# An attention and token-MLP kernel: the opening in pieces of 128 tokens, with two of its eight tiles transposed by DMA

## The chip, the cores and the metric

The kernel runs on one core of one Trainium2 chip. The metric is the device time of one execution in microseconds (us); lower is better. TensorE (PE) multiplies matrices, VectorE (DVE) and ScalarE (ACT) do element-wise work and reductions, GpSimd (POOL) clears buffers and issues transfers, SyncE (SP) issues transfers only. SP, ACT and POOL each have a queue of transfers; all queues are served by the same 16 DMA engines of the core.

## What is computed

Four layers in a row: twice an attention block and a token-mixing MLP, each with a layer norm in front and a residual sum behind.

```python
x = A_x                                              # (1, 2048, 1024) bf16
x = x + _A_ref(_layernorm(x), A_wqkv, A_wo)          # attention
x = x + _B_ref(_layernorm(x), B_w1, B_b1, B_w2, B_b2)  # token MLP
x = x + _A_ref(_layernorm(x), A_wqkv, A_wo)
x = x + _B_ref(_layernorm(x), B_w1, B_b1, B_w2, B_b2)

# _A_ref: H = 32 heads of 32, W = 8 keys a query, dilation 2
idx = pos[:, None] - (jnp.arange(W) * 2)[None, :]    # keys at s, s-2, ..., s-14
logits = einsum("bhsd,bhswd->bhsw", q, k[..., idx, :]) * Dh ** -0.5
attn = softmax(where(idx >= 0, logits, -1e9))
o = einsum("bhsw,bhswd->bhsd", attn, v[..., idx, :]) @ wo

# _B_ref: mixes along the 2048 tokens
u = gelu(einsum("bsd,sf->bdf", h, w1) + b1);  y = einsum("bdf,fs->bds", u, w2) + b2
```

## The kernel before

The dilation of 2 splits the 2048 tokens into two classes, even and odd tokens, which never meet in the attention. Each class has 1024 tokens: eight tiles of 128 tokens (NT = 8), or two halves of 512 (HT). The attention of a class needs the normalized input transposed, with features on the partitions: `hT[c][hf]` holds class c, token half hf, so tiles 0 to 3 of class 0 are in `hT00` and tiles 4 to 7 in `hT01`.

The change touches the opening of the first attention layer. There the eight class-0 tiles of x are loaded (`x_stage`, L247: even tiles on SP's queue, odd tiles on ACT's) into buffers called gg. For each tile, DVE computes mean and variance (`moments`, L264), ACT the reciprocal root (`rsqrt`, L197), DVE normalizes in place (`norm`, L273); for tile 4, called `own`, ACT does all of it (`own_sum`, `own_square`, `norm_act`). TensorE then turns the tile in eight transpositions of 128x128 into a PSUM bank (`turn`, L287) and DVE or ACT copies it into hT (`place`, L292). Matmuls on the identity (`idle`, L258) fill TensorE's time before there is work. The program order of TensorE, DVE, ACT and POOL in this opening is written out by hand in `first_tiles` (L251); SP's order follows from when each transfer is asked for.

A projection is one unit of `project(c, part, dt, hf)` (L407): part 0, 1 or 2 for q, k or v, dt one of eight groups of 128 features, hf the token half. It is eight matmuls of 128x512 over the features (or over fewer columns, `lo` to `hi`, when called in pieces), and then an ACT copy into q, k or v. Its weights are loaded on SP's queue when the first unit asks (`weights`, L378). In the hand-written part, half 0 of k 0, k 1, q 0, q 1, k 2 and k 3 is projected, then half 1 of k 0, k 1, q 0 and q 1. Half 1 is the first reader of hT01.

After the opening, `qk` (L440) multiplies q by the shifted k on DVE, 4096 elements per partition at a time, into a tile T, and TensorE sums each head with a selection matrix (`qk_sum`, L475) into the bank sc. For the first head group (n = 0) the four T's of a pair are each followed by their own sums. When all sums of a group are there, `softmax_front` (L485) and `softmax_back` (L495) run on ACT and DVE; the probabilities go through DRAM to be spread over partitions (`spread`), and `pv` multiplies them with v.

The eight class-1 tiles are loaded by POOL into the same gg buffers, each into one that held a class-0 tile: tile i of class 1 takes the place of tile (i + 7) mod 8 of class 0 (`staged`, L243). So the first of them waits for TensorE's transposition of tile 7. They are normalized by DVE (even) and ACT (odd) and transposed by DMA on SP's queue (`to_hT`, L240). The biases b1 and b2 of the MLP are loaded by POOL (`load_biases`, L156), two bytes at a time, ahead of these tiles; they are used only in the MLP.

The rest is laid out by a planner, `weave` (L792): it walks through the attention's units in order, keeps an estimate of the time on TensorE and on DVE, and pulls units from fill streams ("second" for class 1's tiles, "v_ahead", "out0" and others) when TensorE would wait. A unit `("at", pe, dve)` sets the planner's two clocks, `("drain", name)` takes all that is left of a stream. These numbers only decide order.

Of the kernel before, what the change touches and what calls it, by code (L numbers as in the profile page):

```python
# [11 lines left out]
ALU = mybir.AluOpType  # L12
# [14 lines left out]
def kernel(  # L27
# [42 lines left out]
    AHEAD = 5.0  # L70
    assert D == H * DH and W == 8 and SC == 1024 and HD * KD == H and SB * CH == 32
# [67 lines left out]
    sel = const.tile([P, SB * DQ, 32], BF16, name="sel")  # L139
    nc.gpsimd.memset(sel[:], 0.0)  # L140
# [5 lines left out]
    maskc = const.tile([P, W, W], FP32, name="maskc")  # L146
# [4 lines left out]
    b1_bf = const.tile([P, FT], BF16, name="b1_bf")  # L151
    b2_bf = const.tile([P, NT, DIL], BF16, name="b2_bf")
    b1_sb = const.tile([P, FT], FP32, name="b1_sb")
    b2_sb = const.tile([P, NT, DIL], FP32, name="b2_sb")
# [92 lines left out]
    def x_stage(c, i):  # L247
        eng = nc.gpsimd if c else (nc.scalar if i % 2 else nc.sync)
        eng.dma_start(out=staged(c, i), in_=xin_v[c, i])

    def first_tiles(hT, project):  # L251
        tiles = [staged(0, i) for i in range(NT)]
        mv, rs, tps = {}, {}, {}
        s1, t1, nm, ss = (st(n, [P, w]) for n, w in (("s1", NDC), ("t1", 1), ("nm", 1), ("ss", 1)))
        junk = x2("junk")
        own = NT // 2

        def idle(n):  # L258
            ps = bank()
            for _ in range(n):  # L260
                nc.tensor.matmul(ps[:].rearrange("p (b t) -> p b t", t=P), lhsT=ident[:],
                                 rhs=ident[:].unsqueeze(1).to_broadcast([P, 4, P]), start=True, stop=True)

        def moments(i):  # L264
            s = st("bn", [P, NDC, 6])
            for n in range(NDC):
                nc.vector.bn_stats(out=s[:, n, :], in_=tiles[i][:, n * 512:(n + 1) * 512])
            mv[i] = st("mv", [P, 2])
            nc.vector.bn_aggr(out=mv[i][:], in_=s[:])
            rs[i] = st("rs", [P, 1])  # L270
            rsqrt(rs[i][:], mv[i][:, 1:2], 1.0, eps1)

        def norm(i):  # L273
            norm_dve(tiles[i], tiles[i], mv[i][:, 0:1], rs[i])

        def own_sum(n):
            nc.scalar.activation(out=junk[:, n * 512:(n + 1) * 512], in_=tiles[own][:, n * 512:(n + 1) * 512],
                                 func=ACT.Identity, accum_out=s1[:, n:n + 1])

        def own_square():  # L280
            nc.scalar.activation(out=t1[:], in_=s1[:, 1:2], func=ACT.Copy, scale=-1.0 / D)  # L281
            nc.scalar.activation(out=nm[:], in_=s1[:, 0:1], func=ACT.Identity, bias=t1[:], scale=-1.0 / D)
            nc.scalar.activation(out=junk[:], in_=tiles[own], func=ACT.Square, bias=nm[:], accum_out=ss[:])
            rs[own] = st("rs", [P, 1])
            rsqrt(rs[own][:], ss[:], 1.0 / D, eps1)

        def turn(i):  # L287
            tps[i] = psp.tile([P, KD, P], BF16, name="tp", tag="ps")
            for kt in range(KD):
                nc.tensor.transpose(tps[i][:, kt, :], tiles[i][:, kt * P:(kt + 1) * P], ident[:])  # L290

        def place(i, copy):  # L292
            copy(out=hT[0][i // 4][:, :, (i % 4) * P:(i % 4 + 1) * P], in_=tps.pop(i)[:])

        dve, act = nc.vector.tensor_copy, nc.scalar.copy
        idle(16)
        moments(0)
        own_sum(0)
        moments(1)
        norm(0)  # L300
        turn(0)
        idle(3)
        own_sum(1)
        moments(2)
        norm(1)
        turn(1)
        idle(5)
        place(0, act)
        moments(3)
        place(1, dve)  # L310
        norm(2)
        norm(3)
        banks = {}
        for u, i in (((1, 0), 2), ((1, 1), 3), ((0, 0), None)):
            banks[u] = bank()
            project(*u, 0, banks[u], 0, 2 * P)
            if i:
                turn(i)
        own_square()
        place(2, act)  # L320
        place(3, dve)
        norm_act(tiles[own], tiles[own], nm, rs[own])
        moments(own + 1)
        moments(own + 2)
        for n, u in enumerate(banks):
            project(*u, 0, banks[u], 2 * P, HT)
            if n == 0:
                turn(own)
                norm(own + 1)
                place(own, dve)  # L330
                moments(own + 3)
                norm(own + 2)
        for n, u in enumerate(((0, 1), (1, 2), (1, 3))):
            if n == 2:
                norm(own + 3)
            turn(own + 1 + n)
            place(own + 1 + n, dve)
            project(*u, 0, bank(), 0, HT)
        for u in ((1, 0), (1, 1), (0, 0), (0, 1)):
            project(*u, 1, bank(), 0, HT)  # L340

# [15 lines left out]
    class Attn:  # L357

        def __init__(self, li, hT, early):
            self.li, self.hT, self.early = li, hT, early  # L360
            self.oT = [[None] * KD for _ in range(DIL)]
            self.wts = {}
            self.pbs = {}
            self.prior = None

# [41 lines left out]
        def project(self, c, part, dt, hf, ps=None, lo=0, hi=HT):  # L407
# [5 lines left out]
            for kt in range(KD):  # L413
# [4 lines left out]
                nc.tensor.matmul(ps[:, lo:hi], lhsT=cols, rhs=self.hT[c][hf][:, kt, lo:hi], start=(kt == 0), stop=(kt == KD - 1))  # L418
# [21 lines left out]
        def qk(self, n, dq):  # L440
# [10 lines left out]
            for par in range(2):  # L451
                if not joined:
                    yield "dve", 2.2, ready, free if par else [], 0.0, 0.0
                    yield "pe", 0.6, [], [], 0.0
                T = self.t_buf(n, dq, par)
                mult = nc.vector.tensor_tensor(out=T, in0=q.unsqueeze(1).to_broadcast([P, 4, SC]),  # L456
                                               in1=window(k, par, 2, [(2, 4), (1, SC)]), op=ALU.mult)
# [4 lines left out]
                if not joined:  # L462
                    self.qk_sum(dq, par, T)
# [5 lines left out]

        def t_buf(self, n, dq, par):  # L470
            if self.li == 0 and 0 < n < 3:
# [76 lines left out]
        def stream(self, lead):  # L548
# [39 lines left out]
            if lead is not None:  # L588
                yield "drain", "second"
            yield "open", "v_ahead"  # L590
            for n in range(last + 1):
                done = self.early if n == NCQ else 0
                for half in range(2):
                    nx = (n + half, 1 - half)
                    turn = nx == (NCQ, 0) and self.li > 0
                    yield from self.qk(n, 2 * half)
                    yield from self.qk(n, 2 * half + 1)
                    if half:
                        yield from self.softmax_front()
                    if lead is not None and nx == (0, 1):  # L600
                        for u in ((0, 2, 1), (0, 3, 0), (0, 3, 1),):
                            yield from self.proj(0, *u)
                    elif nx[0] <= last and not turn:
# [188 lines left out]
    def weave(lead, fills, lags):  # L792
# [35 lines left out]
        for kind, *unit in lead:  # L828
# [3 lines left out]
            elif kind == "drain":  # L832
                while unit[0] in opened:
# [27 lines left out]
    for li in range(2):  # L861
# [9 lines left out]
        def opening():  # L871
            for i in range(NT):
                x_stage(0, i)
            load_biases()
            clear_pads()
            with tc.manual_schedule(engines={getattr(mybir.EngineType, e) for e in ("PE", "DVE", "Activation", "Pool")}):
                first_tiles(hT, partial(at_.project, 0))
                for i in range(NT):
                    x_stage(1, i)
            yield "at", 27.0, 29.0  # L880
            for u in ((1, 2, 1), (1, 3, 1), (0, 2, 0),):
                yield from at_.proj(0, *u)
# [75 lines left out]
```

## Time and profile before

| | |
|---|---|
| runs, us | 1280.4, 1280.18, 1280.54, 1280.45; median 1280.43 |
| the profiled execution | 1280.4 us, span 1278.6 us from first to last instruction |
| granted TensorE clock | 1.000 |
| DMA moved | 173.00 MB in 217,816 packets |

TensorE's operations in the opening, by line, with the mean time of one (starts lie closer than that, since matmuls are pipelined):

| line | what | count up to 40 us | mean ns |
|---|---|---|---|
| L261 | warm-up on the identity, 512 columns | 24 | 472 |
| L290 | transposition, 128 columns | 64 | 220 |
| L418 | projection, 256 columns | 48 | 273 |
| L418 | projection, 512 columns | 81 (7 to 40 us) | 379 |

Other operations of the first 60 us:

| what | where | us |
|---|---|---|
| half statistics of a tile, two of them | DVE L267 | 1.29 |
| aggregate | DVE L269 | 0.21 |
| normalize a tile | DVE L233 | 0.50 |
| copy a turned tile into hT | DVE L293 / ACT L293 | 0.69 / 0.99 |
| one multiply of q and k, 4096 elements | DVE L456 | 2.28 |
| copy of k or v, 1024 elements; of q, 512 | ACT L425; L422 | 1.00; 0.57 |
| issue of an x tile by POOL | POOL L249 | 0.54 |
| DMA transpose of a tile, issue to landing | SP L241 | 3.1 to 5.9, median 4.6 |

The profile's timeline lists, per engine, the start of a group of equal instructions, its length, engine, line, operation, tiles and count; in brackets the idle time before it and what ended that. L numbers are lines of the kernel. "PEld" is TensorE loading weights, "SPq" the issuing of transfers by SP. Busy TensorE is not TensorE at its peak.

### The profile page before, as it was taken

How to read it: one execution, taken by the hardware profiler on the slowest of the kernel's cores; microseconds unless marked ns; L12 is line 12 of the kernel's file. 1: busy time of each engine (PE TensorE's matmuls, PEld its weight loads, DVE VectorE, ACT ScalarE, POOL GpSimd, SP SyncE). 2: the span in 40 equal slices, each digit the busy share in tenths (PEclk: the TensorE clock that was granted, in tenths of full speed). 3: DMA queues.
4: the chain of work that ended last, by engine and by line, in shares of the span. 5: the costliest groups of instructions: out<-in, count | busy, mean ns of one | idle time of the engine just before them, and what ended most of it. 6: DMA issues, size and time to landing. Idle time of an engine off the chain costs nothing.

```text
span 1278.6 us, 15576 instructions
## 1 busy us (share of the span) xinstructions
PE 1265.0 (99%) x6284; PEld 577.5 (45%) x6284; DVE 689.9 (54%) x869; ACT 489.1 (38%) x812; POOL 61.0 (5%) x166
## 2 busy tenths in 40 slices
PE   8999999999999999999999999999999999999999
PEld 4344444444444444444444444444444444444444
DVE  6789999999114322334798834899930233111011
ACT  6845446634424533324533445453352343000000
POOL 3000001001000000000000000010010000000000
PEclk9999999999999999999999999999999999999999
DMA  9843454553422289953737642358262223344331
GB/s 256 189 124 102 103 139 143 169 144 115 132 83 83 62 233 294 294 159 87 185 105 200 153 124 81 82 156 208 66 181 83 81 67 93 103 129 134 99 115 52
DMA packets 217816, 173.00 MB, mean 135 GB/s; under 512 B 32080, under 2 KB 198352, under 8 KB 215696
## 3 DMA queue, kind: packets, MB, share of 16 engines
q1 hardware_dynamic: 206768, 126.11, 36.6%
q0 software_dynamic: 9248, 37.51, 10.4%
q10 hardware_dynamic: 1728, 8.39, 1.8%
q8 instruction: 49, 0.80, 0.3%
q14 instruction: 23, 0.19, 0.1%
HBM read 139.47 MB, written 26.21 MB: 130 GB/s over the span
## 4 chain that ended last, share of the span: by engine, by line
PE 76%; DVE 5%; issue 2%; ACT 1%; DVEq 0%
PE ps L719 30%; PE ps L743 29%; PE ps L418 11%; PE ps L664 4%; DVE T L456 2%; PE sc L480 1%; DVE pr L538 1%; DVE pr L543 1%; DVE xr L689 0%; ACT h L227 0%; ACT h L238 0%; DVE v L545 0%; DVE xr L692 0%; ACT ln L200 0%; DVE bn L207 0%
## 5 line engine op out<-in xcount | busy, mean ns | idle before, releaser
L719 PE MATMUL ps<-h,w 128*128 128x512 bf16 x1792 | 388.1, 379 | 2.0 <-ACT h L238 2.0
L743 PEld LDWEIGHTS <-w 128*128 128x128 bf16 x1820 | 177.8, 98 | 209.8 <-issue 2.1
L719 PEld LDWEIGHTS <-w 128*128 128x128 bf16 x1792 | 175.1, 98 | 214.2 <-issue 3.4
L418 PE MATMUL ps<-hT,wq 128*128 128x512 bf16 (+1 forms) x1112 | 241.7, 375 | 0.6 <-ACT t L281 0.4
L743 PE MATMUL ps<-g,w 128*128 128x512 bf16 (+1 forms) x1040 | 227.6, 376 | 0.0
L743 PE MATMUL ps<-gg,w 128*128 128x512 bf16 (+1 forms) x780 | 171.8, 376 | 0.0
L748 DVE SCALAR_TENSOR_TENSOR xr<-ps,b_sb,xr 128x512 bf16<-128x512 f32 (+1 forms) x65 | 45.5, 738 | 225.7 <-PE ps L743 193.7
L418 PEld LDWEIGHTS <-wq 128*128 128x128 bf16 x1112 | 109.0, 100 | 128.6 <-issue 8.8
L456 DVE TENSOR_TENSOR T<-q,k 128x4096 bf16<-128x4096 bf16 x44 | 99.0, 2285 | 70.2 <-ACT q L422 52.1
L543 DVE TENSOR_TENSOR pr<-pr 128x2048 bf16<-128x2048 bf16 (+1 forms) x128 | 119.4, 950 | 0.3
L730 DVE TENSOR_TENSOR tmp<-ps,gg 128x512 f32<-128x512 f32 x48 | 33.2, 692 | 150.2 <-PE ps L719 150.2
L418 PE MATMUL ps<-hT,wv 128*128 128x512 bf16 x448 | 100.3, 379 | 0.0
L664 PE MATMUL ps<-wo,oT 128*128 128x512 bf16 x384 | 89.1, 379 | 0.7 <-DVE oT L545 0.7
L425 ACT CAST k<-ps 128x1024 bf16<-128x1024 f32 x60 | 60.7, 1014 | 60.2 <-PE ps L418 58.8
L538 DVE TENSOR_TENSOR pr<-pb,v 128x2048 bf16<-128x2048 bf16 x64 | 75.9, 1218 | 10.8 <-ACT v L425 6.7
L538 DVE TENSOR_TENSOR pr<-pb,g 128x2048 bf16<-128x2048 bf16 x64 | 76.7, 1217 | 7.2 <-DMA pb<-pd 4.6
L418 PEld LDWEIGHTS <-wv 128*128 128x128 bf16 x448 | 48.8, 111 | 48.7 <-issue 4.2
L730 DVE TENSOR_TENSOR tmp<-ps,g 128x512 f32<-128x512 f32 x48 | 33.2, 692 | 49.7 <-PE ps L719 48.7
L664 PEld LDWEIGHTS <-oT 128*128 128x128 bf16 x384 | 37.4, 98 | 46.7 <-DVE oT L545 1.2
L422 ACT CAST q<-ps 128x512 bf16<-128x512 f32 x60 | 34.9, 584 | 49.5 <-PE ps L418 49.5
L731 ACT ACTIVATE gg<-tmp,b_sb 128x512 bf16<-128x512 f32 x48 | 34.6, 722 | 49.9 <-DVE tmp L730 49.9
L774 ACT COPY odd<-w 128x896 bf16<-128x896 bf16 x32 | 30.0, 937 | 55.9 <-DMA w<-in_B_w_dram 55.9
(97 smaller groups left out, 761.5 us busy)
## 6 DMA issues: line engine op xcount, KB each, us to landing
w<-in_B_w_dram SPq DMA_DIRECT2D x56, 512.0 KB, 4.8
w<-in_B_w_dram SPq DMA_DIRECT2D x64, 448.0 KB, 3.8
wq<-in_A_wqkv_dram SPq DMA_DIRECT2D x38, 512.0 KB, 4.2
pb<-pd POOLq DMA_DIRECT2D x16, 1024.0 KB, 8.7
wo<-in_A_wo_dram SPq DMA_DIRECT2D x16, 512.0 KB, 3.8
xa<-xr POOLq DMA_DIRECT2D x32, 256.0 KB, 3.3
xr<-xa SPq DMA_DIRECT2D x32, 256.0 KB, 3.8
wv<-in_A_wqkv_dram SPq DMA_DIRECT2D x14, 512.0 KB, 5.8
```

The source lines that it names most:

```text
L418: nc.tensor.matmul(ps[:, lo:hi], lhsT=cols, rhs=self.hT[c][hf][:, kt, lo:hi], start=(kt == 0), stop=(kt == KD - 1))
L422: nc.scalar.copy(out=self.q_of(c, dt)[:, hf * HT:(hf + 1) * HT], in_=ps[:])
L425: nc.scalar.copy(out=window(buf, 0, PADK + hf * HT, [(KW + 1, 2), (1, HT)]), in_=ps[:].unsqueeze(1).to_broadcast([P, 2, HT]))
L456: mult = nc.vector.tensor_tensor(out=T, in0=q.unsqueeze(1).to_broadcast([P, 4, SC]), in1=window(k, par, 2, [(2, 4), (1, SC)]), op=ALU.mult)
L538: mult = nc.vector.tensor_tensor(out=pr[:, :, u, :], in0=pb[:, :, u, :], in1=window(self.v_of(c, dt), par, 2 + hf * HT, [(TB, 4), (2, 4), ...
L543: nc.vector.tensor_tensor(out=pr[:, :, 0:wd, :], in0=pr[:, :, 0:wd, :], in1=pr[:, :, wd:2 * wd, :], op=ALU.add)
L664: nc.tensor.matmul(banks[(i, n)][:], lhsT=at_.oT[c][kt][:, i * P:(i + 1) * P], rhs=wo_t[n][kt // 4][:, kt % 4, :], start=(kt == 0), stop=( ...
L719: nc.tensor.matmul(ps[:], lhsT=wt[c][:, i, fl * P:(fl + 1) * P], rhs=h2[c][i // 4][:, i % 4, dc * 512:(dc + 1) * 512], start=(k == 0), sto ...
L730: nc.vector.tensor_tensor(out=tmp[:], in0=ps[:], in1=gs, op=ALU.add)
L731: nc.scalar.activation(out=gs, in_=tmp[:], func=ACT.Gelu_apprx_tanh, bias=b1_sb[:, ft:ft + 1])
L743: nc.tensor.matmul(ps[:, 0:xc.stop - xc.start], lhsT=w2t(ft, c), rhs=g[ft // GF][:, ft % GF, xc], start=(ft == 0), stop=(ft == FT - 1))
L748: nc.vector.scalar_tensor_tensor(out=xo[:, xc], in0=ps[:, 0:xc.stop - xc.start], scalar=b2_sb[:, i, c:c + 1], in1=xo[:, xc], op0=ALU.add, ...
```

## The change

The opening is rewritten. Tile 0 is loaded in two halves of 64 rows, on SP's and ACT's queues; the weights of k and q of the first pair are asked for between the x tiles; the biases are loaded after class 1's tiles. The first projections run on 128 tokens (tile 0, then tile 1) and on two tiles after that. Tiles 4 and 5 are no longer turned by TensorE and copied: `turn` returns at once for them, and `place` issues a DMA transpose on SP's queue. The multiplies of q and k of the first pair are split: `multiply_ahead` does three of them for the first 512 tokens as soon as these are projected, and the rest later, each T with its own buffer (one of them in a gg buffer). The order of projections and multiplies in the first head group changes, as do the planner's clocks there, and "drain" may take a number of units.

```diff
+    AHEAD_T = ((0, 0), (0, 1), (1, 0))
...
-    def x_stage(c, i):
-        eng = nc.gpsimd if c else (nc.scalar if i % 2 else nc.sync)
-        eng.dma_start(out=staged(c, i), in_=xin_v[c, i])
+    def x_stage(eng, c, i, part=slice(0, P)):
+        eng.dma_start(out=staged(c, i)[part], in_=xin_v[c, i][part])
...
         def turn(i):
+            if i in (own, own + 1):
+                return
             tps[i] = psp.tile([P, KD, P], BF16, name="tp", tag="ps")
...
         def place(i, copy):
+            if i in (own, own + 1):
+                return to_hT(tiles[i], hT, 0, i)
             copy(out=hT[0][i // 4][:, :, (i % 4) * P:(i % 4 + 1) * P], in_=tps.pop(i)[:])
...
+        banks = {u: bank() for u in ((1, 0), (1, 1), (0, 0), (0, 1))}
+        for u in ((1, 0), (1, 1)):
+            project(*u, 0, banks[u], 0, P)
...
+        for u in ((1, 0), (1, 1)):
+            project(*u, 0, banks[u], P, 2 * P)
         norm(3)
...
+        project(0, 0, 0, banks[(0, 0)], 0, 2 * P)
+        turn(3)
+        stats(own + 1, 0)
         place(3, dve)
+        project(0, 1, 0, banks[(0, 1)], 0, 2 * P)
...
         for n, u in enumerate(banks):
             project(*u, 0, banks[u], 2 * P, HT)
-            if n == 0:
+            if n == 2:
                 turn(own)
-                norm(own + 1)
                 place(own, dve)
...
+        turn(own + 1)
+        place(own + 1, dve)
+        norm(own + 3)
+        project(1, 2, 0, bank(), 0, HT)
+        turn(own + 2)
+        place(own + 2, dve)
+        ps = bank()
+        project(1, 3, 0, ps, 0, 2 * P)
+        turn(own + 3)
+        place(own + 3, dve)
+        project(1, 3, 0, ps, 2 * P, HT)
-        for u in ((1, 0), (1, 1), (0, 0), (0, 1)):
+        for u in ((1, 0), (0, 0), (1, 1), (0, 1)):
             project(*u, 1, bank(), 0, HT)
+        for dq, par in AHEAD_T:
+            ahead(0, dq, par, HT)
...
+        def multiply_ahead(self, n, dq, par, hi):
+            c, dt = n // NCQ, (n % NCQ) * DQ + dq
+            T, lo, mult = self.begun.get((n, dq, par)) or (self.t_buf(n, dq, par), 0, None)
+            if lo < hi:
+                mult = self.multiply(T, self.q_of(c, dt), self.k_of(c, dt), par, lo, hi)
+            self.begun[(n, dq, par)] = T, hi, mult
...
             if lead is not None:
-                yield "drain", "second"
+                for dq, par in AHEAD_T:
+                    self.multiply_ahead(0, dq, par, SC)
+                yield from self.qk(0, 0)
+                for u in ((1, 3, 1), (0, 2, 0)):
+                    yield from self.proj(0, *u)
+                self.multiply_ahead(0, 1, 1, SC)
+                for u in ((0, 2, 1), (0, 3, 0), (0, 3, 1)):
+                    yield from self.proj(0, *u)
+                yield "drain", "second", NT // 2
...
+                    if lead is not None and n == 0:
+                        yield "drain", "second", NT // 4
                     if half:
+                        if lead is not None and n == 0:
+                            yield "at", 39.3, 54.6
                         yield from self.softmax_front()
...
         def opening():
-            for i in range(NT):
-                x_stage(0, i)
-            load_biases()
+            x_stage(nc.sync, 0, 0, slice(0, P // 2))
+            x_stage(nc.scalar, 0, 0, slice(P // 2, P))
+            x_stage(nc.scalar, 0, 1)
+            x_stage(nc.sync, 0, 2)
+            at_.weights(0, 1, 0)
+            x_stage(nc.scalar, 0, 3)
+            x_stage(nc.sync, 0, 4)
+            at_.weights(0, 0, 0)
+            for i in range(5, NT):
+                x_stage(nc.sync, 0, i)
             clear_pads()
...
                 for i in range(NT):
-                    x_stage(1, i)
+                    x_stage(nc.gpsimd, 1, i)
+                load_biases()
```

## The prediction

> **What bounds the kernel now.** I read the page's first two parts, then the waits of TensorE, then TensorE's and the queues' timeline over the first 60 us. The chain of waits is printed only from 202 us on, so it says nothing of the opening.
>
> ```profile
> span 1278.6 us, 15576 instructions
> PE 1265.0 (99%) x6284; PEld 577.5 (45%) x6284; DVE 689.9 (54%) x869; ACT 489.1 (38%) x812; POOL 61.0 (5%) x166
> ```
>
> TensorE is idle for 1278.6 - 1265.0 = 13.6 us in all. So a change of the opening can save only warm-up, idle gaps and work taken off TensorE, and it costs whatever new gap it makes. The timeline of TensorE shows where the opening stands:
>
> ```profile
> 1.56 5.49 PE L261 MATMUL ps<-ident 128*128 128x512 bf16 x16 [1.56 <-POOL ident masks.py:199]
> ...
> 11.95 1.03 PE L418 MATMUL ps<-hT,wq 128*128 128x256 bf16 x8 [0.38 <-ACT t L281]
> ...
> 23.86 1.89 PE L418 MATMUL ps<-hT,wv 128*128 128x512 bf16 x8
> 25.59 4.70 PE L418 MATMUL ps<-hT,wq 128*128 128x512 bf16 x21
> ...
> 39.25 0.61 PE L480 MATMUL sc<-T,sel 128*32 128x512 bf16 x8 [0.87 <-DVE T L456]
> ...
> 52.02 0.61 PE L480 MATMUL sc<-T,sel 128*32 128x512 bf16 x8 [0.71 <-DVE T L456]
> ```
>
> Projections start at 11.95; at 25.59 TensorE turns to token half 1, the first place that reads hT01, into which the change writes by DMA. In both kernels the same six projections of half 0 stand before that place (in another order), so "when does it start" is the measure. Later gaps before 80 us are 0.87, 0.71 and 0.11 (5.00 - 4.89 busy, in the window 70 to 75): 1.69 us. From there to 183 us TensorE has no gap, so a shift at 80 us reaches the end.
>
> The queues decide the rest: the bytes by stretch (last two columns: DMA share, GB/s), and SP's and POOL's issues:
>
> ```profile
> 2.00:11.50 9.50, 7.95 (x40) 3.27 (x38) 6.74 (x15) 3.85 (x13) 6.26 (x50) 1.00 1.01 323
> 11.50:15.50 4.00, 3.62 (x41) 3.16 (x40) 1.92 (x5) 3.81 (x11) 0.00 (x0) 1.00 1.29 67
> 16.00:20.00 4.00, 4.00 (x42) 3.06 (x40) 3.93 (x10) 2.33 (x6) 0.40 (x2) 1.00 1.21 289
> 21.00:24.50 3.50, 3.40 (x28) 1.99 (x28) 2.36 (x5) 3.00 (x6) 0.18 (x1) 1.00 1.08 346
> ```
> ```profile
> 6.01 1.73 POOL L158 DMA_DIRECT2D b_bf<-in_B_b_dram  x1
> 16.38 0.21 POOL L160 CAST b_sb<-b_bf 128x28 f32<-128x28 bf16 x1 [7.00 <-DMA b_bf<-in_B_b_dram]
> 24.32 4.27 POOL L249 DMA_DIRECT2D gg<-in_A_x_dram  x8 [7.48 <-PE tp L290]
> ```
>
> From 11.5 to 15.5 only 67 GB/s move: in the packet records the bias loads (two-byte elements, seen from 11.0, landed at 16.3 and 16.6) run there, and the weight packets beside them take 0.15 to 0.26 us instead of 0.034.
>
> **The change, part by part.**
>
> (a) The earlier start. Tile 0 comes as two halves on two queues. Before, tiles 0 and 1 ran side by side; 262 KB at the 286 GB/s of 2 to 5 us are 0.92 us, so tile 0 is there at 4.63 - 0.92 = 3.7. Then two half-statistics (1.32), aggregate to scale 0.77, normalization 0.50, transposition 0.62: 6.9. DVE gives the next tile 1.87 later (1.32 + 0.13 + 0.42), ACT's copies (0.99) fit between, so the first 128-token projections start near 8.8 instead of 11.95. From there to half 1: six projections of 1.73 (8 x 0.216) and four transpositions of 0.45 are 12.2, so 21.0 at best; DVE's pace, and tile 7's scale, which stands behind four copies on ACT (0.9, 0.9, 0.47, 0.47), add 1 to 2.5. TensorE is free for half 1 at 22.7 (22.0 to 23.5), 2.9 before 25.59. The two transpositions taken off (16 x 0.056 = 0.9) are in this. The split first matmuls cost nothing: a 128-column one takes 0.056, half of 0.11 for 256 columns.
>
> (b) Tiles 4 and 5 by DMA. Both are normalized by about 17.5, but SP issues them behind all weight loads, as its queue's 15th and 16th. Ahead of them in SP's and ACT's queues are eight x tiles and eight loads of 524 KB: 6.29 MB, the same as before. 3.07 MB are moved by 11.5 (9.5 x 323). The bias loads now go last on POOL, so the hole at 67 GB/s goes: the 512-byte loads' rest, 1.65 MB at 289, takes 5.7 and three 1024-byte loads, 1.57 MB at 346, take 4.5: 21.7. Before, one DMA engine lagged 1.2 at this point (last packets 26.2, the others' 25.0), and a transpose stands still while one engine lags (at 725.5 to 726.5); so they start between 21.7 and 22.9. A transpose alone (the two issued at 44.63 and 45.96) streams in 1.4, one that was queued early (issued 50.32) in 1.0, the slowest of these eight in 2.4; landing follows 0.6 after the last packet.
>
> Now a collision. POOL starts class 1's x tiles as soon as TensorE has turned tile 7, near 21.8 instead of 24.02; bytes came 1.2 after issue, so from 23.3. Five of the eight follow at once (the sixth waits for tile 4's transpose): 1.31 MB at 301 GB/s are 4.4 us, on the same 16 engines. No row has a transpose beside a full POOL queue; in the nearest (a store of POOL's beside one at 674 us) it took 2.4 instead of 1.4. Bounds: without lag or collision 21.7 + 2 x 1.0 + 0.6 = 24.3; with POOL's tiles served first 23.3 + 4.4 + 1.0 + 0.6 = 29.3. I take lag, the first done at 24.1, the second at half rate (2 x 1.1 = 2.2) and 0.6: 26.9. TensorE then waits 26.9 - 22.7 = 4.2 us, and half 1 starts at 26.9 instead of 25.59: +1.3. Behind the transposes SP holds two weight loads that wait for half 1 on TensorE anyway; POOL's last three x tiles and the biases wait for the landing, and DVE's statistics of class 1 for them.
>
> The Trainium skill, "Advanced Engine Details and Errata", X-Bar Transpose (TRN2), holds that transposes run about as fast as ordinary DMAs (350 to 400 GB/s); here 188 GB/s moved while one streamed alone, and by the page's rate the second would land near 24.9 (22.9 + 2 x 0.7 + 0.6, an estimate), the sum 2.0 lower.
>
> (c) Multiplies ahead and the new order behind them. DVE can multiply first token halves while TensorE stands, and projections are put before the sums that waited: 0.87 and 0.71 go. In return the pair's sums that open the next head group come one projection (1.73) earlier in TensorE's order, where now they wait 0.11; ACT, full from 30 to 55 us, restarts its copies only after half 1 began, so DVE's softmax before these sums gains less than TensorE. New wait: 0 to 1.6, I take 0.5. Net -1.69 + 0.5 = -1.2 (-1.7 to -0.1).
>
> (d) Moved without cost: the bias loads now disturb queues from about 29 to 35, where next weights and class 1's transposes run. What is late next is class 1's hT, landed at 58.8 and first read near 70.7: some 11 us cover them; without it a hole like the old one costs up to 3. Units shifted one place around 140, 168, 200 and 233 us stand beside waits of 0.30 and 1.17: 0 to 1, taken as 0.2.
>
> Sum: +1.3 - 1.2 + 0.2 = +0.3 on the profiled execution: span 1278.6 and 1.8 around it, 1280.4, which agrees with the median 1280.43. Forecast 1280.7.
>
> **The rivals.**
>
> A, slower: POOL's five tiles go ahead of tile 5's transpose. It lands at 29.3: +3.7 - 1.2 + 0.2 = +2.7, 1283.1; and TensorE stands 6.6 us, so C comes on top: 1285. For it: POOL's packets are 4096 bytes against the transposes' 256, and at 31.5 to 33 us SP's 512-byte packets got about one for each of POOL's. Against: at 674 us nine transpose packets passed for each of POOL's. It decides from a landing after 28.5.
>
> B, faster: no lag and the first transpose's packets are long queued. Landing at 24.3 gives -1.3 - 1.2 + 0.2 = -2.3, 1278.1; if both hide (before 22.7), -2.9 - 1.2 + 0.2 = -3.9, 1276.5. For it: one transpose did stream in 1.0. Against: even 2 x 1.0 from 21.7 is too late to hide.
>
> C, a cold array after the wait. TensorE's first nine matmuls come 0.425 apart, the rest 0.216:
>
> ```profile
> 4.53 0.15 PEld L261 LDWEIGHTS <-ident 128*128 128x128 bf16 x1 [0.28 <-issue]
> 4.95 0.15 PEld L261 LDWEIGHTS <-ident 128*128 128x128 bf16 x1 [0.28 <-issue]
> 5.59 0.96 PEld L261 LDWEIGHTS <-ident 128*128 128x128 bf16 x5
> ```
>
> The weight loads of the warm-up show it: 0.42 between the two single ones, then five in 0.96. That is 9 x 0.21 = 1.9 us lost. No later gap of the trace (longest 1.17) brings it back; one of 4.2 has no row, so 0 to 1.9 and 1282.6 with it. I count it at three in ten for 4.2, likely for 6.6.
>
> The skill's "TensorE: Matmul & The Clock Gate", Part 1, speaks against this change: the clock halves after an idle window of some 3.4 us. No gap here is as long; by that rule the 4.2 us would be paid with 1.9 more.
>
> **How the numbers follow.** Forecast (landing 25.5 to 27.9, no cold array) 0.42: 1279.3 to 1281.7. C at such a landing 0.18: 1281.2 to 1283.6. A 0.27: 1282.5 to 1285.5. B 0.13: 1276.5 to 1279.3. A measurement of this kernel tells 0.2% (2.6 us) from no change: below 1277.9 or above 1283.0. Faster: most of B, 0.10. Slower: a third of C, 0.06, and nine tenths of A, 0.25: 0.31, raised to 0.36 since a second lagging engine isn't counted. Same: 0.54. Range 1277.6 to 1285.3; it leaves out B's hidden end and A with a longer wait. The likeliest case's own range is 1279.3 to 1281.7.
>
> **What would show it.** First projections near 8.8; no stretch at 67 GB/s before 20 us; a TensorE gap of about 4 us ended by a DMA of hT, half 1 at 26.9; no gaps of 0.87 and 0.71 later. Matmuls 0.425 apart after the gap mean C; a landing after 28.5, with POOL's tiles landed first, A; no gap, B. A gap before 22 us, or one over 1 us after 60 us, would prove (a) or (c) wrong.

## The result and the profile after

The changed kernel takes 1287.03 us in the median of 34 executions (1278.54 to 1293.98), the kernel before 1280.5 (54 executions, 1279.87 to 1282.24). The ratio is 1.0042, 95% interval 1.0033 to 1.0051: slower by more than the 0.2% that a measurement can tell. The executions of the changed kernel scatter over 15 us where those of before keep within 2.4 in this comparison. 26 of 35 (the profiled one included) lie above 1285, the others near 1278.5 to 1282.5. 29 of the 35 show a granted TensorE clock below 1.000; of the kernel before it is 6 of 103 in the comparisons below, the slowest of them at 1284.55. So the time now depends on chance in a way that it hardly did before. The profiled execution, 1286.56 us with a span of 1284.5, is one of the common kind.

The page after: span, busy time of the engines, and TensorE's granted clock in the 40 slices.

```profile
span 1284.5 us, 15601 instructions
...
PE 1264.8 (98%) x6293; PEld 578.2 (45%) x6293; DVE 689.5 (54%) x870; ACT 489.4 (38%) x812; POOL 62.3 (5%) x166
...
PEclk9999899999999999999999999999999999999999
```

TensorE is busy as long as before (1264.8 against 1265.0), so in the sum all that was added is idle time: 19.7 us in place of 13.6. The equal busy times hide an exchange: there is less warm-up and transposing, and some matmuls run at half the clock, 2.5 us as worked out below. One clock digit is below 9, in the fifth slice (128 to 161 us), far behind the opening. TensorE's waits up to 260 us (in total, times, longest):

```profile
PE ps L451 <- DMA wv<-in_A_wqkv_dram: 4.6, 1, 4.6
PE tp L301 <- DVE gg L235: 3.0, 4, 1.5
...
PE ps L451 <- DMA hT<-gg: 1.5, 1, 1.5
```

The wait that I forecast, on hT, is there with 1.5 us. The one that decides is a single wait of 4.6 us on a weight load. TensorE's timeline, opening first (start, length, line, operation, count, idle time before and what ended it):

```profile
8.26 0.62 PE L301 MATMUL tp<-ident,gg 128*128 128x128 bf16 x8 [1.48 <-DVE gg L235]
...
10.26 0.62 PE L301 MATMUL tp<-ident,gg 128*128 128x128 bf16 x8 [0.72 <-DVE gg L235]
10.71 1.06 PE L451 MATMUL ps<-hT,wq 128*128 128x128 bf16 x16
...
25.89 7.07 PE L451 MATMUL ps<-hT,wq 128*128 128x512 bf16 x32 [1.50 <-DMA hT<-gg]
...
68.59 1.05 PE L531 MATMUL sc<-gg,sel 128*32 128x512 bf16 x16
...
130.24 12.21 PE L451 MATMUL ps<-hT,wv 128*128 128x512 bf16 x44 [4.55 <-DMA wv<-in_A_wqkv_dram]
```

Half 1 starts at 25.89 instead of 25.59 and the gaps of 0.87 and 0.71 are gone. The sums at 68.59 stood at 72.62 before:

```profile
72.62 1.05 PE L480 MATMUL sc<-gg,sel 128*32 128x512 bf16 x16
```

One projection (8 x 0.216 = 1.73) now stands behind them instead of ahead, so the lead there is 4.03 - 1.73 = 2.3 us. Then 4.55 us are lost at once, and more behind it. TensorE's weight loads after the wait:

```profile
130.24 0.15 PEld L451 LDWEIGHTS <-wv 128*128 128x128 bf16 x2 [5.03 <-DMA wv<-in_A_wqkv_dram]
130.66 0.15 PEld L451 LDWEIGHTS <-wv 128*128 128x128 bf16 x1 [0.27 <-issue]
131.08 0.15 PEld L451 LDWEIGHTS <-wv 128*128 128x128 bf16 x1 [0.28 <-issue]
...
135.35 6.63 PEld L451 LDWEIGHTS <-wv 128*128 128x128 bf16 x31 [0.28 <-issue]
```

Twelve steps of 0.426 from 130.24 to 135.35, then 0.216 again: 12 x 0.21 = 2.5 us lost at half clock. The clock record has 0.5 from 128.6 to 135.4. So -2.3 + 4.55 + 2.5 = +4.75 of the +5.9 by which the span grew; of the other 1.15 us, 0.8 is idle time after 140 us, in small waits that I didn't follow.

Why is that load late? SP's issues and POOL's around it, after:

```profile
114.50 3.82 SPq L429 DMA_DIRECT2D wq<-in_A_wqkv_dram  x2
120.54 0.37 SPq L429 DMA_DIRECT2D wv<-in_A_wqkv_dram  x1
```
```profile
115.34 0.62 POOL L557 DMA_DIRECT2D pd<-Pb  x1 [45.65 <-DVE Pb L553]
120.50 0.51 POOL L571 DMA_DIRECT2D pb<-pd  x1 [4.54 <-DMA pd<-Pb]
```

and before:

```profile
122.85 0.37 SPq L396 DMA_DIRECT2D wv<-in_A_wqkv_dram  x1
```
```profile
119.38 0.62 POOL L506 DMA_DIRECT2D pd<-Pb  x1 [45.35 <-DVE Pb L502]
125.05 0.51 POOL L520 DMA_DIRECT2D pb<-pd  x1 [5.05 <-DVE pr L538]
```

The tile wv holds weights of v, pb the probabilities on their way back from DRAM (pd). Before, the load of wv (524 KB in packets of 1024 bytes; the second half of the weights of class 0's v 4 to 7) has 2.2 us on the queues before POOL's load of pb (1 MB in packets of 8192 bytes) joins. It lands 5.7 us after issue (at 128.57) and TensorE never waits. After, both are issued within 0.04 us, pb first. From 124 to 128 us, 124 packets of wv (some 0.08 us each) and 95 of pb (0.58 each) are served: nearly one for one, with bytes 1 to 6 in favour of pb. wv lands 9.7 us after issue, at 130.20. POOL's chain (pd) moved up 4.04 us, SP's load 2.31; the difference is 1.73, one projection (the other 0.5 of the lost lead is pd, which landed that much sooner). The planner, set to ("at", 39.3, 54.6), puts one class-1 projection fewer ahead of the pair's sums. This wv load waits for a weight buffer to come free, which the order of projections sets; pd, and pb behind it, wait for the sums and the softmax.

The shift costs the load twice. TensorE's use of wv moved up with the sums and not with SP's issue. After, TensorE asked for it at 125.69 (130.24 - 4.55), 5.15 us after the issue; before, the same matmul, the 37th of its group, started at 129.56, 6.71 after it. The difference is again about one projection. So the load has less time, and more company, at once.

### The profile page after: what moved, and what is told of

It reads as the page before. It is cut to its first block, busy times and chain, and to the rows that moved or that the text cites. A ratio compares the mean times of both kernels' runs of the same rounds, so it can differ in the third digit from the quotient of the medians.

```text
span 1284.5 us, 15601 instructions
## 1 busy us (share of the span) xinstructions
PE 1264.8 (98%) x6293; PEld 578.2 (45%) x6293; DVE 689.5 (54%) x870; ACT 489.4 (38%) x812; POOL 62.3 (5%) x166
## 3 DMA queue, kind: packets, MB, share of 16 engines
HBM read 139.47 MB, written 26.21 MB: 129 GB/s over the span
## 4 chain that ended last, share of the span: by engine, by line
PE 75%; DVE 5%; ACT 2%; issue 1%; DMA 1%; DVEq 0%
PE ps L780 29%; PE ps L804 29%; PE ps L451 11%; PE ps L725 4%; DVE T L509 2%; PE sc L531 1%; DVE pr L589 1%; DVE pr L594 1%; DVE xr L750 1%; DMA hT<-hb 1%; ACT h L229 0%; ACT h L240 0%; ACT ln L202 0%; ACT k L458 0%; DVE xr L753 0%
## 5 line engine op out<-in xcount | busy, mean ns | idle before, releaser
L451 PE MATMUL ps<-hT,wq 128*128 128x512 bf16 (+2 forms) x1136 | 241.2, 370 | 2.2 <-DMA hT<-gg 1.5
L509 DVE TENSOR_TENSOR T<-q,k 128x4096 bf16<-128x4096 bf16 (+1 forms) x45 | 97.1, 2191 | 71.4 <-ACT q L455 52.5
L451 PE MATMUL ps<-hT,wv 128*128 128x512 bf16 (+1 forms) x456 | 102.9, 382 | 4.6 <-DMA wv<-in_A_wqkv_dram 4.6
L451 PEld LDWEIGHTS <-wv 128*128 128x128 bf16 x456 | 50.2, 112 | 54.6 <-issue 6.7
```

The costliest lines, as they stand in the source:

```text
L451: self.last_mm = nc.tensor.matmul(ps[:, lo:hi], lhsT=cols, rhs=self.hT[c][hf][:, kt, lo:hi], start=(kt == 0), stop=(kt == KD - 1))
L509: return nc.vector.tensor_tensor(out=T[:, :, lo:hi], in0=q[:, lo:hi].unsqueeze(1).to_broadcast([P, 4, hi - lo]), in1=window(k, par, 2 + lo ...
```

## The experiments

Times are medians; "before" was run beside them on the same chip (1280.5 to 1280.8). "Full clock" counts executions with a granted clock of 1.000.

| kernel | us | ratio to before, 95% interval | full clock |
|---|---|---|---|
| the changed kernel | 1287.03 | 1.0042 (1.0033 to 1.0051) | 6 of 35 |
| order_back | 1281.22 | 1.0001 (0.9992 to 1.001) | 2 of 10 |
| tensore_turns | 1286.73 | 1.0043 (1.0023 to 1.0063) | 0 of 8 |
| before_shifted | 1288.5 | 1.0044 (1.0024 to 1.0065) | 4 of 10 |
| pb_after_wv | 1280.48 | 1.0002 (0.9993 to 1.0011) | 3 of 10 |
| after_filled | 1285.95 | 1.0047 (1.0029 to 1.0065) | 4 of 9 |
| tensore_order | 1278.8 | 0.9989 (0.9977 to 1.0) | 7 of 10 |
| order_warm | 1281.48 | 1.0007 (0.9997 to 1.0016) | 4 of 10 |
| tensore_order_warm | 1278.52 | 0.9983 (0.9973 to 0.9992) | 10 of 10 |
| before_dma_turns | 1289.64 | 1.0069 (1.0054 to 1.0084) | 0 of 4 |
| order_filled | 1282.03 | 1.0012 (1.0003 to 1.0022) | 9 of 10 |
| t_on_act | 1280.45 | 1.0001 (0.9992 to 1.001) | 6 of 10 |
| bias_early | 1279.53 | 0.9989 (0.998 to 0.9999) | 10 of 10 |
| pool_after_t | 1283.21 | 1.0013 (1.0003 to 1.0022) | 2 of 10 |
| norm_first | 1278.26 | 0.998 (0.9971 to 0.9989) | 10 of 10 |

**order_back.**

```diff
-                            yield "at", 39.3, 54.6
+                            yield "at", 38.3, 54.6
```

> The changed kernel with one number of the planner altered: its clock is set to 38.3 instead of 39.3 us, which puts one more class-1 projection ahead of the pair's sums, so that TensorE's order from the first class-1 projection on is that of the kernel before. Theory S (the shift by one projection brings POOL's load of pb and SP's load of wv together): no wait on wv near 126 us, clock 1.00 throughout, the 2.3 us gained by the first 70 us stay: 1277.5 to 1279.5, ratio 0.998 to 0.9995. Rival L (the two added DMA transposes have turned SP's queue and its eight completion lanes against POOL's): the order of projections does not matter, the wait of 4.6 us stays: 1286 to 1288.

The wait on wv is gone and none of its ten executions is above 1285 (the highest is 1284.3). SP's and POOL's issues in its timeline:

```profile
121.32 0.37 SPq L429 DMA_DIRECT2D wv<-in_A_wqkv_dram  x1
```
```profile
122.96 0.51 POOL L571 DMA_DIRECT2D pb<-pd  x1 [4.49 <-DMA pd<-Pb]
```

wv is 1.64 ahead again. One number of the planner is worth 5.8 us. The 2.3 us gained were not all kept, though: 1281.2 against 1277.5 to 1279.5 expected, and a clock below 1.000 in eight of ten. Something else still cost 2 to 3 us.

**tensore_turns** takes the two transposes by DMA out and leaves the order shifted.

```diff
         def turn(i):
-            if i in (own, own + 1):
-                return
...
         def place(i, copy):
-            if i in (own, own + 1):
-                return to_hT(tiles[i], hT, 0, i)
```

> The changed kernel with tiles 4 and 5 transposed by TensorE again, everything else kept (the shifted order too). S: the opening moves by less than 1 us (16 transpositions of 0.056 us come back, the wait of 1.5 us goes), and the wait on wv and the half clock stay: 1285.5 to 1288.5. L: with the two transposes out of SP's queue the wait goes: 1277.5 to 1279.5.

The wait stays and is longer. TensorE's waits, and its issues of wv and pb at 120.83 and 120.94:

```profile
PE ps L447 <- DMA wv<-in_A_wqkv_dram: 7.2, 1, 7.2
```
```profile
120.83 0.37 SPq L425 DMA_DIRECT2D wv<-in_A_wqkv_dram  x1
```
```profile
120.94 0.51 POOL L567 DMA_DIRECT2D pb<-pd  x1 [4.68 <-DMA pd<-Pb]
```

So the late wait comes without the transposes; rival L falls.

**before_shifted** makes the shift alone, in the kernel before.

```diff
+                        if lead is not None and n == 0:
+                            yield "at", 39.3, 54.2
                         yield from self.softmax_front()
```

> The kernel before with a planner's clock set (39.3, 54.2) ahead of its first softmax, which takes one class-1 projection out from between later sums: from the tenth projection after that on TensorE's order is that of the changed kernel; the opening and both queues' opening loads stay those of before. S: a wait of 4 to 5 us on wv near 128 us with about 12 matmuls at half clock behind it, so 7 us more: 1286 to 1289. L: nothing to collide, 1280 to 1281.

Seven of ten executions are above 1285 and the median rises by 7.9 us. The profiled one, of 1281.26, is among the three that escaped: SP issues wv at 123.50 and POOL pb at 123.60, yet wv lands 4.5 us later and TensorE doesn't wait. With issues about 0.1 us apart the landing came 4.5 us after the issue here, 9.7 in the changed kernel and 12.4 in tensore_turns: a race that either side can win, which fits the scatter of the changed kernel.

**pb_after_wv** keeps the shifted order and takes away the collision alone.

```diff
-                nc.gpsimd.dma_start(out=pb[:]..., in_=src)
+                load = partial(nc.gpsimd.dma_start, out=pb[:]..., in_=src)
...
+                        follow(self.held(), wv, mybir.DependencyClass.Sync)
```

> The changed kernel with its shifted order, but POOL's two loads of pb for the second head group are issued only once SP's wv load of 120.5 us has landed. S: alone on the queues wv lands 4 to 5 us after its issue, before TensorE asks for it; no wait, no half clock: 1277.5 to 1280 (pb lands some 3 us later, which VectorE can stand). Rival W (wv is late by itself, since its buffer is released too late): the wait stays, or shrinks by less than half: 1284 or more.

Without pb beside it wv lands 3.7 us after its issue (121.72 to 125.38). POOL's issue stands behind it:

```profile
125.93 0.51 POOL L437 DMA_DIRECT2D pb<-pd  x1 [8.77 <-DMA wv<-in_A_wqkv_dram]
```

No wait on wv, and no execution above 1283.4. The buffer is released in time, though TensorE wants the tile just as soon as in the changed kernel (5.2 us after the issue); it is the company on the queues that makes wv late. The median, 1280.48, is a little above what was expected, with clocks below 1.000 in seven of ten; the transposes by DMA are still in this kernel.

**after_filled** puts work in place of the idle time.

```diff
+                if (self.li, c, part, kt) == (0, 0, 2, KD // 2) and dt // DQ == 1 and not self.filled:
+                    self.filled = True
+                    warm = bank()
+                    for _ in range(20):
+                        nc.tensor.matmul(warm[:]..., lhsT=ident[:], rhs=ident[:]..., start=True, stop=True)
```

> The changed kernel with 20 matmuls of the identity matrix (20 x 0.216 = 4.3 us) put on TensorE just before the matmul that waits for wv near 126 us; their result is not used. Theory C (the half clock after the wait comes from TensorE standing idle): the wait shrinks to the part beyond 4.3 us, no half clock near 130 us, so the executions that collided lose the 2.5 us less (1287.0 becomes about 1284.5) and those that did not collide pay 4.3 more: median 1283 to 1286, no execution with a clock below 0.998. Rival (the half clock is imposed whatever TensorE does): clock 0.997 stays in most executions, 1286.5 to 1289.

Inconclusive. Four executions at full clock took 1283.4 to 1284.7, but five had lower clocks and 1286 to 1292.7 (two of them below the 0.998 that was expected as the lowest), and the profiled one had no wait on wv at all. A wait can outlast the filler (7.2 us in tensore_turns), so this doesn't tell whether idling alone halves the clock.

**tensore_order, order_warm, tensore_order_warm** look for what order_back still loses: the transposes, the shortened warm-up, or both. tensore_order is order_back with tensore_turns' edit; order_warm adds

```diff
-        idle(14)
+        idle(20)
...
-        idle(3)
+        idle(6)
```

and tensore_order_warm has all three.

> The changed kernel with the planner's clock at 38.3 (order of before) and with tiles 4 and 5 transposed by TensorE. If the two DMA transposes cost what order_back's profile shows (a wait of 2.6 us on hT, less the 0.9 us of TensorE's transpositions), this is 0.5 to 1.7 us below order_back's 1281.2: 1279.5 to 1280.7, with a clock of 0.999 in most executions as in order_back. Rival (the transposes are hidden in the median execution): within 0.4 of order_back.

> order_back with 20 and 6 warm-up matmuls of the identity in the opening in place of 14 and 3. Theory F (most executions of the new opening fall to half clock for one period of 3.4 us near 11 us, because TensorE stands idle 1.5 and 0.7 us there; clock 0.999 in 8 of order_back's 10 executions): clock 1.000 in nearly all, 1.7 us less than order_back in the median: 1279.0 to 1280.0, and less scatter. Rival (the scatter comes from the landing of the transposes): clocks and median as in order_back, 1281 to 1281.7.

> All three: order of before, tiles 4 and 5 by TensorE, 20 and 6 warm-up matmuls. If S, F and the price of the DMA transposes all hold, the terms add: 1281.2 - 1.7 - (0.5 to 1.7) = 1277.8 to 1279.0, clock 1.000, faster than before by 1.4 to 2.6 us. If F falls: as tensore_order.

The transposes are it: without them 1278.8, below the expected range, and seven of ten at full clock where I had expected most below it. Its profiled execution, at 1283.93 the slowest of the ten, still waits for wv, though pb was issued 1.82 us behind it:

```profile
130.68 9.56 PE L447 MATMUL ps<-hT,wv 128*128 128x512 bf16 x36 [3.28 <-DMA wv<-in_A_wqkv_dram]
```

With the transposes, more warm-up changes nothing (1281.48), so theory F falls as the main cause. order_warm's timeline shows where its clock goes:

```profile
27.69 4.85 PE L451 MATMUL ps<-hT,wq 128*128 128x512 bf16 x11 [3.85 <-DMA hT<-gg]
```

and its clock record is 0.5 from 25.9 to 32.7. All three edits together give the best kernel so far, 1278.52, at full clock in all ten, 2.3 us below the 1280.82 of before. Half 1 starts there at 24.27.

**before_dma_turns** is tensore_turns' edit the other way round, in the kernel before.

> The kernel before with only one part of the change: tiles 4 and 5 transposed by DMA through SP's queue; opening, bias loads and order stay. Theory D (the transposes land behind all of SP's weight loads, 1.2 to 3.4 us after TensorE is free, and the wait makes a half clock in part of the executions): the loads of before end at 25.0 to 26.2 us, the second landing is at 28 to 29.5 instead of a start at 25.59, so +2.7 to +3.9, and 1.7 more where the clock falls: 1283 to 1286, clock 0.999 or less in half or more of the executions. Rival H (the transposes cost little, the 2.7 us between order_back and tensore_order come from the new opening around them): 1280 to 1281.5.

It costs 9.1 us in the median of four executions, far more than expected. TensorE's timeline:

```profile
33.43 9.39 PE L422 MATMUL ps<-hT,wq 128*128 128x512 bf16 x31 [8.21 <-DMA hT<-gg]
```

In the packet records tile 5's transpose runs from 27.9 to 31.0 among POOL's tiles, which POOL issued from 23.79 on, and lands only at 33.3; the clock is 0.5 for 10.2 us. This is my rival A, with four of POOL's five tiles landed first, and C on top. The profiled execution of the changed kernel escapes it narrowly: its transposes end at 25.20 and POOL's first tile packet comes at 25.24.

**order_filled** sets filler into the wait on hT.

```diff
+        idle(12)
         for u in ((1, 0), (0, 0), (1, 1), (0, 1)):
             project(*u, 1, bank(), 0, HT)
```

> order_back with 12 matmuls of the identity (12 x 0.216 = 2.6 us) on TensorE between its last projection of half 0 (about 24.4 us) and half 1; their result is not used. TensorE then can't start half 1 before about 27.0, later than order_back's profile (26.67). Theory C (idling there costs the clock): clock 1.000 in nearly all executions and 1279.4 to 1280.8, so not above order_back's 1281.2 though work was added. Rival (the clock does not depend on that wait, or the landings scatter beyond it): 0.999 in most executions, 1281.5 to 1283.

Nine of ten at full clock, against two of ten: the half clock of order_back comes from standing idle before half 1. The time doesn't follow, 1282.03: its profile has 1.9 us of waits of the sums on DVE's T up to 60 us where order_back's has none of note. The edit moved more than it said: with the filler, VectorE's order has two more of class 1's tiles (statistics and a normalization) ahead of the second multiply, which starts at 32.58 instead of 29.64. So the clock is answered here, and the time not.

**t_on_act** issues the transposes on another queue.

```diff
-                return to_hT(tiles[i], hT, 0, i)
+                return nc.scalar.dma_start_transpose(out=hT[0][1][...], in_=tiles[i])
```

> order_back with the two transposes issued on ScalarE's queue, which is empty since about 9 us, in place of SP's, where they stand behind the weight loads. Theory Q (their place in SP's queue is what makes them late): they stream from about 17.5 us on beside the loads, landing 20 to 23, no wait on hT, half 1 at about 24.4, clock 1.000: 1278 to 1279.6, if the loads that they slow are not needed at once. Rival R (the transposes themselves are slow beside other transfers, wherever they are issued): landing after 25, waits on hT as before or new ones on weights: 1280.5 to 1284.

Rival R. The first transpose, issued at 18.34 (for 1.34 us), moves its first packet at 21.49, as on SP's queue (21.50 in order_back), gets 506 of its 1024 packets through by 23.0 beside the last weight packets, and the second lands at 26.02. Half 1 starts at 26.16. The place in SP's queue isn't what makes them late. (Six of ten executions keep full clock against order_back's two, and the median is 0.8 lower; the intervals are the same.)

**bias_early** undoes the move of the bias loads in the best kernel.

```diff
+            load_biases()
             clear_pads()
...
                     x_stage(nc.gpsimd, 1, i)
-                load_biases()
```

> tensore_order_warm with the bias loads back at their place of before, right behind the x tiles, in place of behind class 1's tiles. If moving them was worth something on the path, the stretch of some 4 us at 67 GB/s comes back near 11 to 15 us and the weights of half 0 or half 1 are waited for: 1279.5 to 1282. If not (the weights have that much slack): 1278.2 to 1279.

From 11 to 15 us 103 GB/s move instead of 322, DVE waits 2.41 us for a tile of x and TensorE behind it:

```profile
18.17 2.78 PE L447 MATMUL ps<-hT,wq 128*128 128x256 bf16 x24 [1.97 <-DVE hT L302]
```

The median rises by 1.0 us; the two intervals overlap, so the size is uncertain, but the place of the wait is not.

**pool_after_t** keeps POOL's tiles off the transposes' end.

```diff
-                    x_stage(nc.gpsimd, 1, i)
+                    follow(x_stage(nc.gpsimd, 1, i), turned[-1], mybir.DependencyClass.Sync)
```

> order_back with POOL's loads of class 1's tiles held until the second transpose (tile 5) has landed. In the profiles so far that transpose's last packet is at 25.2 to 25.6 us in four kernels alike, but it lands 0.55 us later in one and 1.9 later in another, where POOL's packets begin about 0.1 us before its end. Theory P (the landing waits behind POOL's tile packets): landing 0.5 to 0.6 after the last packet, half 1 at 25.7 to 26.2, a wait of 1.3 to 1.8, clock 1.000 in most executions: 1279.0 to 1280.2 against order_back's 1281.2. Rival (the landing scatters by itself, or a wait of 1.5 is already enough for the half clock): 0.999 in most executions, 1280.8 to 1281.8.

Half right at most. The second transpose lands 0.46 us after its last packet (25.75 to 26.21), as theory P says, where order_warm's took 1.9 (25.61 to 27.55). But in order_filled and pb_after_wv POOL's packets had also begun before the last one, and the landing took 0.55; so theory P isn't settled by this. POOL also issues class 1's tiles 3.4 us later than in order_back (26.88 against 23.47), and VectorE, whose order is fixed, waits for one of them. VectorE's waits from 30 to 50 us:

```profile
DVE bn L209 <- DMA gg<-in_A_x_dram: 4.5, 1, 4.5
```

A multiply of q and k behind it starts at 46.50 instead of 43.12, and TensorE waits for that:

```profile
26.34 7.07 PE L454 MATMUL ps<-hT,wq 128*128 128x512 bf16 x31 [1.92 <-DMA hT<-gg]
...
48.84 1.04 PE L534 MATMUL sc<-T,sel 128*32 128x512 bf16 x8 [2.73 <-DVE T L512]
```

with the clock at 0.5 from 48.1 to 55.0. The wait moved and the time rose to 1283.2.

**norm_first** tests why the first projections were late.

```diff
         root(0)
-        stats(1, 0)
         norm(0)
+        stats(1, 0)
```

> tensore_order_warm with tile 0's normalization put ahead of the first half-statistic of tile 1 on VectorE; in the changed kernel it stands behind that statistic, which waits for tile 1 until 7.06 us. Theory N (this order is what held the first projections at 10.7 where 8.8 was predicted): tile 0 normalized about 6.3 instead of 7.7, transposed near 7 to 8 behind the 20 warm-up matmuls, the first projections 0.4 to 1.3 us earlier (9.4 to 10.3) as VectorE still needs tile 1's two statistics after 7.06; half 1 0.3 to 0.6 earlier; 1278.0 to 1278.4. Rival (TensorE is held by VectorE's whole chain of statistics, not by this one wait): first projections as before within 0.3, 1278.4 to 1278.9.

In the changed kernel VectorE's timeline has tile 0's normalization behind a statistic of tile 1:

```profile
7.06 0.69 DVE L268 BATCH_NORM_STATS2 bn<-gg 128x6 f32<-128x512 bf16 x1 [1.40 <-DMA gg<-in_A_x_dram]
7.67 0.53 DVE L235 TENSOR_SCALAR gg<-gg,mv,rs 128x1024 bf16<-128x1024 bf16 x1
```

With the two exchanged it runs at 6.22, but TensorE is then held by its own warm-up (to 8.8) and the first projections come at 10.98, no earlier than the 10.68 of tensore_order_warm. The median, 1278.26, is not told apart from 1278.52. The pair isn't clean: tile 1 landed at 7.09 here and at 6.04 in the other profile. What it does show is that the order of these two operations alone moves nothing.

## Why the prediction was wrong

The forecast was 1280.7 with a range to 1285.3; measured 1287.03, above it. By its steps:

(a) The earlier start. I expected first projections near 8.8; they came at 10.71. In TensorE's order they stand behind tile 1's transposition (10.26), and I had let tile 1 follow tile 0 by VectorE's 1.87 us without asking when it lands. It landed at 7.04; VectorE stood idle 1.40 us for it, and tile 0's normalization stood behind that. Undoing the order alone didn't help (norm_first). TensorE was free for half 1 at 24.4, not 22.7.

(b) The transposes. The first was done at 24.17 (24.1 predicted), the second landed at 25.76 in the profile (26.9), and half 1 started +0.3 late instead of +1.3. POOL's tiles came at 25.24, not 23.3, since TensorE was later. But the single profile flatters it: with the order fixed, the transposes cost 2.4 us in the median (1281.22 against 1278.8). The landing follows the last packet by 0.46 to 0.57 us where POOL is quiet (pool_after_t, the changed kernel), as I had it (0.6); where POOL's packets come in it is 0.55 in two profiles, but 1.2 in order_back, 1.9 in order_warm and 2.3 in before_dma_turns. That term isn't the constant that I took it for.

(c) The gaps. Net -1.2 predicted; from the start of half 1 to the pair's sums the kernel before took 72.62 - 25.59 = 47.03, the changed one 68.59 - 25.89 + 1.73 = 44.43, so -2.6. The 1.69 of gaps went with no new wait, and 0.9 of busy time with them; TensorE now turns from projections to sums at five places there instead of seven, which I take for the reason and didn't test.

(d) This is the step that failed. "Units shifted one place ... stand beside waits of 0.30 and 1.17: 0 to 1, taken as 0.2." I had seen that the pair's sums come one projection earlier, and priced it only by TensorE's own waits. I didn't look at what the shift does to the distance between two transfers on different queues: SP's wv and POOL's pb, 2.2 us apart before and 0.04 after; nor at the time between SP's issue and TensorE's use of the tile, 6.7 us before and 5.15 after. order_back and before_shifted show that the shift makes the wait, and pb_after_wv that it takes pb's company. How much of it the shorter time alone would cost no run separates: in ten of the eleven profiles with a lead of 1.5 to 2.4 us wv landed 5.3 to 7.0 after its issue, which against 5.15 would be 0.2 to 1.9 us of waiting (an estimate). Price of the whole: 4.55 + 2.5 = 7.05 us in the profile, 7.9 in the median when made alone (before_shifted). The sum's other terms were on the safe side: up to 70 us the profiled execution led by 2.3 where I forecast a loss of 0.1.

The bias loads: I counted their move as removing the stretch at 67 GB/s, and bias_early shows the stretch, and a wait behind it, come back.

The rivals: A did not happen in the profile of the changed kernel but does, nearly, in before_dma_turns; B's early landing (24.3) came nowhere. C, the cold array, was the right mechanism at the wrong place: I gave it to the wait on hT, where order_warm's profile has it and where order_filled puts it for order_back, and the profiled execution of the changed kernel paid it at 130 us: 2.5 us behind a wait of 4.55, where I had reckoned 1.9. The rule that I cited from the Trainium skill ("TensorE: Matmul & The Clock Gate", Part 1), half clock after an idle window of some 3.4 us, fits that wait; the last section has shorter ones that halved the clock too. My last sentence on what would show it, that a gap over 1 us after 60 us would prove (a) or (c) wrong, named the sign but not the step.

## What to carry to other kernels

When a change shifts the order of one engine by one unit, list the transfers whose issue hangs on different events (here a buffer released by TensorE and a result from VectorE) and compare their distance before and after: two loads that were 2 us apart and are now issued together can cost more than the whole change was about. Compare too how long each load has from its issue to its first use. A load that TensorE needs soon should not meet one with larger packets: here holding the other back took the wait away (pb_after_wv), while a lead of 1.8 us helped in most profiles and not in all (tensore_order). And a single profile isn't the kernel: the scatter of the executions and their clocks told here that something was left to chance, before any trace did.

## What was not expected of the hardware

The half clock comes in steps. The clock records have it for 3.41, 6.83 or 10.24 us, once, twice and three times 3.413, and within a run all its changes lie on one grid of that step. The length of a wait alone doesn't decide: half clock came behind waits of 3.28 (tensore_order), 3.85 (order_warm), 4.55 (the changed kernel), 7.25 (tensore_turns) and 8.21 (before_dma_turns), but also behind one of 2.73 (pool_after_t) and behind two gaps of 1.18 and 0.72 (pb_after_wv), and a wait of 3.79 (after_filled, on hT) passed without any.

The grid tells more. Each of these seven half clocks began at the end of a step in which TensorE was busy for 1.51 us or less: 0.51 in the changed kernel, 0.26 in tensore_order, 0.71 in before_dma_turns, 0.88 in tensore_turns, 1.33 in order_warm, 1.40 in pool_after_t, 1.51 in pb_after_wv. It ended with the first step that was busy for 3.29 us or more; steps with 2.48 or less left it at half. The wait of 3.79 fell across two steps, with 1.49 and 1.38 us of work in them, and the clock held, as it did behind steps of 1.36 (order_back) and 1.49 (pool_after_t). So in these profiles the border lies near 1.4 to 1.5 us of work in a step, and how a wait falls on the grid counts as well as its length. The Trainium skill ("TensorE: Matmul & The Clock Gate", Part 1) says that the window runs freely, at 3413 ns. The records agree on the step; a free run would also explain why near-equal waits differ.

The 16 parts of one load can land far apart. Those of wv in tensore_turns came from 124.00 to 133.18, all but two by 125.83; in tensore_order fifteen were there by 125.64 and the last at 130.64. The last part decides when the load counts as there. In the changed kernel all sixteen came late and close together, from 129.02 to 130.20. So a late wv has two forms in these profiles, and the medians don't tell how often each comes.
